# Attention summary of batches 1 to 3: exponentials transposed in blocks by VectorE, four chunks weighed over 128 rows

## The chip, the cores and the metric

One core of one Trainium2 chip. The metric is the device time of one execution in microseconds, lower is better; the figure of a kernel is the median of its runs.

## The reference

There are 4 batches of 12480 tokens with 128 channels, and 32 inducing rows that all batches share. First, in each batch, the inducing rows attend to the tokens and give a summary h of 32 rows; then the tokens attend to h. The result goes through a layer of 2048 hidden units with a piecewise quadratic in the middle.

```python
def mab(q, kv):
    s = scale * (q @ kv.transpose(0, 2, 1))
    s = s - s.max(-1, keepdims=True)
    a = np.exp(s)
    a /= a.sum(-1, keepdims=True) + 1e-09
    return a @ kv
h = mab(I, x)            # summary: (B, 32, 128)
y = mab(x, h)            # (B, 12480, 128)

h = y @ w_in             # (49920, 2048)
g = np.where(h >= 1, h, np.where(h <= -1, 0.0, (h + 1) ** 2 / 4.0))
out = g @ w_out          # (49920, 128)
```

The weights w_in and w_out come as 64-bit floats and are converted on the chip.

## The kernel before

**Chunks.** A batch is 26 chunks of 480 tokens (`chunk`). For a chunk, eight steps k each take two blocks of 128 hidden units. TensorE multiplies the attention weights `aT` with `hw`, the product of the summary and w_in, into two banks of PSUM (`hidden`, L943). ScalarE takes Relu(h+1) of it (`rise`, L951) and squares that (`square`, L937); VectorE joins the branches (`bound`, L956), which frees the banks. `rise` and `bound` do both banks in one instruction of 960 columns where the banks are neighbours and both are ready, else in two halves. In six of the eight steps (`SPLIT`) the product with w_out is taken in rounded parts: an upper part `hi` by VectorE (L979), ScalarE (L976) or GpSimd (L974), a lower part `lo` by GpSimd (L982), and three products for each block (L1008). In the other two it is one matmul in full float32. After the eight steps VectorE transposes the sum (L1020) and four DMAs store it (L1024).

**Attention of the tokens** (`attend`) runs in groups of four chunks, 32 rows of partitions for each chunk; the last group of a batch has two.

**Summary** (`summarize`) of a batch also runs in seven groups of four chunks, ahead of that batch: batch 0 at the start, batches 1 to 3 beside the chunks of the batch before. For a group of batches 1 to 3:

- `load`: one DMA for each chunk brings its tokens in rows of 120 partitions (L498, tile `xn`), and four more bring them for the transposed copy (L525, tile `xr`), which VectorE makes in blocks of 32x32 (L528).
- `score`: four matmuls give the scores of four chunks in four quadrants of 32 partitions (L547); VectorE takes the largest of each row (`most`, L552) and scales it (L555); ScalarE takes the exponentials with that offset and sums them (L564). Each chunk has an offset of its own, which the end of the summary sets right.
- `gather`: TensorE transposes the exponentials (`turn`, L588, four instructions for a group), ScalarE or VectorE evicts them (`put`, L596), sixteen matmuls weigh the tokens (`weigh`, L604), each over the 120 tokens of one chunk, and ScalarE keeps the result (`keep`, L611).
- After seven groups a chain of small steps `c1` to `c12` (L645 to L690) joins them into h.

**Order.** Nothing is ordered at run time. `Plan.order` builds the whole program as a list: every operation has a cost, a lag and a due time. The planner walks through time, and each free engine takes the ready operation with the earliest due time. Operations share slots (`SLOTS`: seven banks of PSUM `h`, tiles `xn`, `w`, `hi`, `lo` and so on). Due times are a base, such as 1950 ns for each step, plus a number from the table `DUE`. Every engine, and the queue of DMAs that SP issues, then runs its list strictly in order. Where TensorE would be idle near the start, fillers are put (`keep_on`, L1035).

**The start** loads batch 0 and both weights (L498 and L393). ScalarE, VectorE and GpSimd convert the weights, and VectorE's steps of that are L403, L406, L412, L418 and L423.

## Time and profile before

| | |
|---|---|
| median of 3 runs | 1732.89 us (1730.05 to 1733.73) |
| profiled execution | 1733.12 us, its span 1731.2 us |
| granted TensorE clock, mean | 0.996 |
| busy, share of the span | PE 98%, PEld 72%, DVE 94%, ACT 96%, POOL 94% |
| instructions | PE 8100, DVE 2123, ACT 2453, POOL 879 |

PE is TensorE's matmul, PEld its weight load, DVE VectorE, ACT ScalarE, POOL GpSimd, and SPq the queue of DMAs that SP issues. Times are from the start of the span. "Idle before" names what an engine waited for. The chain of waits goes back from the last instruction, at each step to what released it, and gives the shares of the span by engine.

### The profile page before, as it was taken

The page shows a single profiled execution, that of the slowest core. Times are in us where ns is not written, and L with a number is a line of the kernel's source. Part 1 is how long each engine was busy: PE and PEld are TensorE (multiplying, and loading weights), DVE is VectorE, ACT ScalarE, POOL GpSimd, SP SyncE. Part 2 cuts the span into 40 slices and gives each one's busy share as a digit, 9 for nine tenths or more (in the row PEclk, how much of TensorE's full clock was granted, in tenths as well). Part 3 has the DMA queues.
Part 4 walks back from the last instruction along what each step waited for, and adds up shares of the span by engine and source line. Part 5 has one row for each costly group of instructions (what it writes and reads, how often), then busy time and mean ns, then how long its engine had stood idle before and what let it go on. Part 6 is the DMA issues. An engine that isn't in the chain of part 4 may idle for free.

```text
span 1731.2 us, 26016 instructions
## 1 busy us (share of the span) xinstructions
PE 1702.3 (98%) x8100; PEld 1242.9 (72%) x8100; DVE 1625.2 (94%) x2123; ACT 1662.0 (96%) x2453; POOL 1619.2 (94%) x879
## 2 busy tenths in 40 slices
PE   7999999999999999999999999999999999999998
PEld 5777777777777777767767777777777777777776
DVE  4899999999999999999999999999999999999997
ACT  5699999999999999999999999999999999999997
POOL 1599999999899999999989999999999999999998
PEclk9899999999999999999999999999999999999999
DMA  8543334233343243342143333232212111111111
GB/s 210 136 75 69 67 60 81 48 63 62 62 83 60 51 79 65 64 80 56 36 85 63 73 65 71 51 66 52 44 27 59 35 31 29 34 35 35 34 30 18
DMA packets 427948, 105.74 MB, mean 61 GB/s; under 512 B 370562, under 2 KB 421218, under 8 KB 427810
## 3 DMA queue, kind: packets, MB, share of 16 engines
q1 hardware_dynamic: 427714, 103.96, 30.7%
q8 instruction: 64, 1.05, 0.3%
q14 instruction: 74, 0.61, 0.1%
q10 hardware_dynamic: 96, 0.13, 0.0%
HBM read 48.94 MB, written 25.56 MB: 43 GB/s over the span
## 4 chain that ended last, share of the span: by engine, by line
PE 72%; ACT 9%; DVE 8%; issue 4%; POOL 3%; DMA 2%; SPq 1%; POOLq 0%; DVEq 0%; ACTq 0%
PE banks L1008 49%; PE banks L943 16%; ACT w L951 5%; DVE w L956 4%; ACT w L937 4%; POOL lo L982 3%; DVE hi L979 2%; PE banks L604 1%; PE banks L757 1%; PE banks L547 1%; PE banks L507 1%; DMA xr<-in_x 1%; DVE oT L1020 1%; PE banks L588 1%; PE banks L1035 1%
## 5 line engine op out<-in xcount | busy, mean ns | idle before, releaser
L982 POOL TENSOR_TENSOR lo<-w,hi 128x960 fp32r<-128x960 f32 x624 | 1399.7, 2276 | 40.7 <-DVE hi L979 21.3
L956 DVE SCALAR_TENSOR_TENSOR w<-banks,w 128x480 f32<-128x480 f32 (+1 forms) x1158 | 957.0, 863 | 36.6 <-ACT w L937 30.2
L951 ACT ACTIVATE w<-banks 128x480 f32<-128x480 f32 (+1 forms) x1320 | 841.9, 711 | 16.6 <-PE banks L943 15.1
L937 ACT ACTIVATE w<-w 128x960 f32<-128x960 f32 x832 | 843.2, 1046 | 3.2
L943 PE MATMUL banks<-aT,hw 128*128 128x480 f32 x1664 | 592.3, 425 | 5.3 <-DVE w L956 3.1
L1008 PE MATMUL banks<-hi,w_lo 128*128 128x480 f32 x1248 | 520.6, 417 | 4.7 <-DVE oT L1020 3.6
L979 DVE TENSOR_REDUCE hi<-w 128x960 fp32r<-128x960 f32 x410 | 466.1, 1142 | 19.3 <-PE banks L1008 1.3
L1008 PE MATMUL banks<-hi,w_hi 128*128 128x480 f32 x1248 | 473.4, 379 | 0.0
L943 PEld LDWEIGHTS banks<-aT,hw 128*128 128x128 f32 x1664 | 305.6, 188 | 158.6 <-DVE w L956 74.0
L1008 PE MATMUL banks<-lo,w_hi 128*128 128x480 f32 x1248 | 398.8, 396 | 0.7 <-POOL lo L982 0.5
L1008 PE MATMUL banks<-w,w_f 128*128 128x480 f32 x832 | 395.3, 565 | 0.0
L1008 PEld LDWEIGHTS banks<-hi,w_lo 128*128 128x128 f32 x1248 | 234.8, 188 | 87.8 <-issue 26.4
L1008 PEld LDWEIGHTS banks<-lo,w_hi 128*128 128x128 f32 x1248 | 230.7, 188 | 73.6 <-issue 23.1
L1008 PEld LDWEIGHTS banks<-hi,w_hi 128*128 128x128 f32 x1248 | 234.7, 188 | 53.0 <-issue 22.0
L1008 PEld LDWEIGHTS banks<-w,w_f 128*128 128x128 f32 x832 | 156.1, 189 | 46.8 <-issue 27.2
L974 POOL TENSOR_SCALAR hi<-w 128x960 fp32r<-128x960 f32 x143 | 142.9, 1006 | 5.1 <-PE banks L943 1.2
L1020 DVE STREAM_TRANSPOSE oT<-banks 128x480 f32<-128x480 f32 x104 | 70.2, 675 | 9.9 <-PE banks L1008 9.5
L976 ACT CAST hi<-w 128x960 fp32r<-128x960 f32 x71 | 71.5, 1008 | 6.3 <-DVE w L956 2.3
L528 DVE STREAM_TRANSPOSE xT<-xr 128x480 f32<-128x480 f32 x78 | 51.2, 660 | 1.8 <-DMA xr<-in_x 1.8
L434 POOL TENSOR_TENSOR w_in_sb<-hi,lo 128x256 f32<-128x256 f32 x8 | 6.9, 862 | 39.8 <-DVE hi L423 39.8
L800 POOL TENSOR_TENSOR a<-a,ahi 128x480 fp32r<-128x480 f32 (+1 forms) x28 | 34.6, 1235 | 0.0
L552 DVE TENSOR_REDUCE mg<-banks 128x1 f32<-128x480 f32 (+1 forms) x28 | 18.1, 647 | 16.0 <-PE banks L547 16.0
(107 smaller groups left out, 609.7 us busy)
## 6 DMA issues: line engine op xcount, KB each, us to landing
out<-oT SPq DMA_DIRECT2D x416, 60.0 KB, 2.2
xn<-in_x SPq DMA_DIRECT2D x91, 240.0 KB, 4.4
xr<-in_x SPq DMA_DIRECT2D x312, 60.0 KB, 2.5
aT<-ahi SPq DMA_DIRECT2D x206, 60.0 KB, 2.0
aT<-a SPq DMA_DIRECT2D x206, 60.0 KB, 2.0
w<-in_moe_w_in SPq DMA_DIRECT2D x8, 256.0 KB, 3.6
w<-in_moe_w_out SPq DMA_DIRECT2D x8, 256.0 KB, 5.2
hw<-hy SPq DMA_DIRECT2D x32, 64.0 KB, 2.0
```

The costliest lines, as they stand in the source:

```text
L528: nc.vector.transpose(make(xT[b, c]), xr.tile.rearrange("c n i -> c (n i)"))
L800: nc.gpsimd.tensor_sub(a.tile.bitcast(F32R)[:rows], a.tile[:rows], a_hi.tile[:rows].bitcast(F32))
L937: nc.scalar.activation(w.tile, w.tile, AF.Square, scale=0.5)
L943: nc.tensor.matmul(make(h)[:, :CW], hw[b][ft // 4].tile[:, ft % 4 * P : (ft % 4 + 1) * P], aT[b, c].tile, start=True, stop=True,)
L951: each(of, i, hs_, w, lambda to, h: nc.scalar.activation(to, h, AF.Relu, bias=1.0))
L956: lambda to, h: nc.vector.scalar_tensor_tensor(to, h, 1.0, to, op0=ALU.max, op1=ALU.min),
L974: nc.gpsimd.tensor_scalar(make(hi), w.tile, 1.0, 0.0, op0=ALU.mult, op1=ALU.add)
L976: nc.scalar.copy(make(hi), w.tile)
L979: nc.vector.tensor_reduce(make(hi), w.tile.unsqueeze(3), axis=AX.X, op=ALU.max)
L982: nc.gpsimd.tensor_sub(make(lo), w.tile, hi.tile.bitcast(F32))
L1008: nc.tensor.matmul(acc.tile[:, :CW], wt[k][:, i, :], g.tile[:, i, :], start=first, stop=(acc.parts == 0),)
L1020: nc.vector.transpose(make(oT).rearrange("c n i -> c (n i)"), acc.tile[:, :CW])
```

## The change

It has four parts, all in batches 1 to 3 but the third and fourth.

**1. The summary of batches 1 to 3.** The tokens of the four chunks of a group are loaded into one tile, each chunk in its own 32 partitions, 15 tokens in each partition. The exponentials are transposed by VectorE in blocks of 32x32 (`over`) in place of TensorE's transposes and their eviction. Fifteen matmuls (`weigh_all`) then each weigh 128 rows, which hold tokens of all four chunks. So the four chunks need one common maximum for each inducing row. The four quadrants' maxima are moved beside each other by four DMAs of 32x1 (`line`), reduced (`one_most`) and moved back to the four quadrants by four DMAs (`spread`), and only then scaled (`less`) for the exponential. The first token loads wait for batch 0's last groups, since they share their tile with batch 0's loads.

**2. The table.** `DUE` has new numbers in nearly every line and new rows for the groups' begin (`G`) and weighing (`W`), and some assumed costs change, so the whole order is another one. The split of a step into rounded parts can be done inside PSUM in the new code (`KEPT`), but the table for it is empty and no step does so.

**3. The last chunk** splits five steps and not six (`END`).

**4. The last four stores** go two by two through the SP queue and ScalarE's queue.

```diff
+END = (0, 1, 3, 4, 6)
+KEPT = {}
 SLOTS = dict(
-    h=7, o=1, xn=9, xT=26, ...
+    h=7, o=1, xn=3, x3=9, xT=26, ...
 )
 DUE = {
-    "h": [-29500, -8350, -85150, -9450, -9450, -2350, -58850, -34750],
+    "h": [-32850, -7650, -16250, -11800, -23400, -2500, -53600, -37900],
...
+    "G": [-1550, 51230, 105810, 151540, 201470, 251300, 307230],
+    "W": [26826, 84806, 164936, 190366, 243946, 298076, 350756],
...
-KEEP = 0
+KEEP = 800
-WAIT = 181850
+WAIT = 210850
...
+    tokens = work.tile([P, SLOTS["xn"], 3 * 5 * C], F32, name="tokens")
...
 def load(g, due, step):
...
-                pool = FIRST[c % len(FIRST)] if b == 0 else "xn"
-                xn[c] = in_turn(pool) if pool == "xn" else Slot(pool)
-                got[c] = add(
-                    "SP", 700 if b else 1080, 3000, at(due, "x") if b else at(0, "x0", c),
-                    lambda c=c: nc.sync.dma_start(make(xn[c], [TP, T, C], F32), rows_of[b, c]), [], [xn[c]],
-                )
...
+                else:
+                    xn[c] = xn[c - 1] if q else in_turn("xn")
+
+                    def fetch(c=c, q=q):
+                        t = xn[c].tile or make(xn[c])
+                        nc.sync.dma_start(t[q * M : (q + 1) * M], x_cols[b, c])
+
+                    got[c] = add("SP", 700, 3000, at(due, "x"), fetch, state["first"], [xn[c]])
...
 def score(g, due):
...
             def most():
-                nc.vector.tensor_reduce(
-                    mg[:rows, g : g + 1], p1.tile[:rows, :CW], axis=AX.X, op=ALU.max
-                )
+                to = mq[:rows] if b else mg[:rows, g : g + 1]
+                nc.vector.tensor_reduce(to, p1.tile[:rows, :CW], axis=AX.X, op=ALU.max)
+                if b == 0:
+                    less()
+
+            def line(q):
+                nc.sync.dma_start(m4[:, q : q + 1], mq[q * M : (q + 1) * M])
+
+            def one_most():
+                nc.vector.tensor_reduce(m4[:, Q:], m4[:, :nq], axis=AX.X, op=ALU.max)
+
+            def spread(q):
+                nc.sync.dma_start(mg[q * M : (q + 1) * M, g : g + 1], m4[:, Q:])
+
+            def less():
                 nc.vector.tensor_scalar(nb[:rows], mg[:rows, g : g + 1], -SCALE, None, op0=ALU.mult)
...
-                    to = make(e1[g])[:rows].rearrange("w (i n) -> w i n", i=M)
-                    of = p1.tile[:rows, :CW].rearrange("w (n i) -> w i n", i=M)
+                    to, of = make(e1[g])[:rows], p1.tile[:rows, :CW]
...
+                l = [add("SP", 610, 2700, SC[1], lambda q=q: line(q), [v]) for q in range(nq)]
+                v = add("DVE", 75, 215, SC[1], one_most, l)
+                l = [add("SP", 610, 2700, SC[1], lambda q=q: spread(q), [v, prior]) for q in range(Q)]
+                mosts.extend(l)
+                v = add("DVE", 75, 215, SC[1], less, l)
...
 def gather(g, due, scored):
...
+            if b:
+                def over():
+                    to = make(eN[g], [P, NB, M])[:rows].rearrange("p n m -> p (n m)")
+                    nc.vector.transpose(to, e1[g].tile[:rows])
+
+                def weigh_all():
+                    p = make(ph)
+                    for n in range(NB):
+                        nc.tensor.matmul(
+                            p[n % Q * M : (n % Q + 1) * M, :C], eN[g].tile[:rows, n, :], xn[g * Q].tile[:rows, n, :],
+                            start=n < Q, stop=n >= NB - Q,
+                        )
+
+                def keep_all():
+                    nc.scalar.copy(hs[:, g, :], ph.tile[:, :C])
...
 def chunk(b, c):
...
+            split = k in (END if (b, c) == (B - 1, NCH - 1) else SPLIT)
...
         for k in range(Q):
-            add("SP", 640, 3000, at(due, "o") + 5000, lambda k=k: store(k), [f], [oT])
+            engine = "ACT" if (b, c) == (B - 1, NCH - 1) and k % 2 else "SP"
+            add(engine, 640, 3000, at(due, "o") + 5000,
+                lambda k=k, queue=nc.scalar if engine == "ACT" else nc.sync: store(k, queue), [f], [oT])
```

Counted over the whole order of each engine, the change has these differences: on TensorE 84 transposes of exponentials in batches 1 to 3 fewer, 315 weighing matmuls for 312 in those batches, and 68 fillers for 81; on VectorE 482 double `bound` for 506 and 700 halves for 652, 404 upper parts for 410, and six evictions of exponentials fewer; on ScalarE fifteen of these evictions fewer, 77 upper parts for 71, 339 double `rise` for 344 and 986 halves for 976; on GpSimd 623 lower parts for 624 and 142 upper parts for 143; on the SP queue 162 small DMAs more. TensorE changes 142 times between its two ways of dividing its columns after the first hidden-layer matmul, in both orders.

Three places show what moved. In them `hi`, `lo` and `w` are buffers that the start also uses for converting weights.

VectorE, in a group of batch 1, before (L552 is `most`, L555 its scaling, L956 `bound`, L979 an upper part, L528 the transposed copy, L786 a step of `attend`):

```order
L552 TENSOR_REDUCE mg<-banks 128x1
L555 TENSOR_SCALAR nb_0_118<-mg 128x1
L956 SCALAR_TENSOR_TENSOR w_1562<-banks,w_1562 128x480 x2
L979 TENSOR_REDUCE hi_1601<-w_1541 128x960
L956 SCALAR_TENSOR_TENSOR w_1585<-banks,w_1585 128x960
L786 RECIPROCAL sm_109<-sm_109 128x15
L528 STREAM_TRANSPOSE xT_1619<-xr_1418 128x480
```

The same in the change (L576 is `most`, L585 `one_most`, L591 `less`, L629 `over`, L1022 `bound`, L1080 an upper part, L550 the transposed copy, L1121 the output's transpose):

```order
L576 TENSOR_REDUCE mq_0_135<-banks 128x1
L1022 SCALAR_TENSOR_TENSOR w_1556<-banks,w_1556 128x480 x2
L1080 TENSOR_REDUCE hi_1588<-w_1530 128x960
L1022 SCALAR_TENSOR_TENSOR w_1570<-banks,w_1570 128x480 x2
L550 STREAM_TRANSPOSE xT_1608<-xr_1424 128x480
L1022 SCALAR_TENSOR_TENSOR w_1591<-banks,w_1591 128x960
L585 TENSOR_REDUCE m_1_0_136<-m_1_0_136 32x1
L550 STREAM_TRANSPOSE xT_1623<-xr_1461 128x480
L1022 SCALAR_TENSOR_TENSOR w_1597<-banks,w_1597 128x480 x2
L1080 TENSOR_REDUCE hi_1647<-w_1597 128x960
L1121 STREAM_TRANSPOSE oT_1653<-banks 128x480
L1022 SCALAR_TENSOR_TENSOR w_1630<-banks,w_1630 128x480 x2
```

The scaling stood right behind the maximum. Now five rows stand between `most` and `one_most`, five between that and `less`, which comes next.

The SP queue, at the last loads of batch 0, before (L498 loads tokens, of batch 0 where it is 96x640 and of batch 1 where it is 120x4x128; L393 loads weights):

```order
L498 DMA w_643<-in_x 96x640
L393 DMA w_663<-in_moe_w_out 128x512
L498 DMA xn_684<-in_x 120x4x128
L393 DMA w_696<-in_moe_w_out 128x512
L498 DMA xn_709<-in_x 120x4x128
L498 DMA xn_736<-in_x 120x4x128
L393 DMA w_742<-in_moe_w_in 128x512
L498 DMA xn_757<-in_x 120x4x128
L393 DMA w_768<-in_moe_w_out 128x512
L498 DMA xn_793<-in_x 120x4x128
L498 DMA xn_802<-in_x 120x4x128
L498 DMA xn_815<-in_x 120x4x128
```

The same in the change (L513 loads tokens of batch 0, L521 of batch 1, L408 weights):

```order
L408 DMA w_574<-in_moe_w_out 128x512
L513 DMA tokens<-in_x 96x640 x2
L408 DMA w_628<-in_moe_w_out 128x512
L513 DMA w_646<-in_x 96x640
L408 DMA w_664<-in_moe_w_in 128x512
L408 DMA w_678<-in_moe_w_out 128x512
L408 DMA w_720<-in_moe_w_out 128x512
L408 DMA w_751<-in_moe_w_out 128x512
L408 DMA w_806<-in_moe_w_out 128x512
L408 DMA w_817<-in_moe_w_out 128x512
L408 DMA w_856<-in_moe_w_out 128x512
L521 DMA tokens<-in_x 32x1920 x7
```

Token loads of batch 1 stood among those of w_out; now they stand behind all of them, and two loads of w_out stand ahead of the last load of batch 0.

VectorE, from the first chunk's attention weights on, before (L892 makes these weights; L403 to L423 convert w_out; L763 to L772 are steps of `attend`):

```order
L892 TENSOR_TENSOR aT_982<-banks,aT_982 64x480
L423 SCALAR_TENSOR_TENSOR hi_923<-w_882,hi_923 128x256
L406 TENSOR_SCALAR lo_999<-hi_954 128x256
L403 TENSOR_SCALAR hi_967<-hi_967 128x256
L412 SCALAR_TENSOR_TENSOR lo_999<-w_894,lo_999 128x256
L406 TENSOR_SCALAR lo_1015<-hi_967 128x256
L418 TENSOR_SCALAR hi_954<-lo_999 128x256
L763 STREAM_TRANSPOSE banks<-banks 128x480
L423 SCALAR_TENSOR_TENSOR hi_954<-w_894,hi_954 128x256
L769 TENSOR_REDUCE mx_104<-banks 128x15
L956 SCALAR_TENSOR_TENSOR w_1008<-banks,w_1008 128x960
```

The same in the change (L956 makes the weights, L1022 is `bound`, L827 to L858 are steps of `attend`):

```order
L956 TENSOR_TENSOR aT_1048<-banks,aT_1048 64x480
L827 STREAM_TRANSPOSE banks<-banks 128x480
L833 TENSOR_REDUCE mx_120<-banks 128x15
L836 TENSOR_TENSOR s_202_1084<-banks,mx_120 128x480
L844 TENSOR_REDUCE sm_121<-s_202_1084 128x15
L1022 SCALAR_TENSOR_TENSOR w_1071<-banks,w_1071 128x960
L850 RECIPROCAL sm_121<-sm_121 128x15
L1022 SCALAR_TENSOR_TENSOR w_1080<-banks,w_1080 128x960
L858 STREAM_TRANSPOSE a_1143<-s_202_1084 128x480
L1080 TENSOR_REDUCE hi_1149<-w_1080 128x960
```

The conversions that stood behind the first chunk's weights are gone from there; they stand ahead of them.

## Rows read from the trace of the kernel before

**Rows 1.** The page, parts 1 and 4: busy time, share and count; chain by engine.

```profile
PE 1702.3 (98%) x8100; PEld 1242.9 (72%) x8100; DVE 1625.2 (94%) x2123; ACT 1662.0 (96%) x2453; POOL 1619.2 (94%) x879
...
PE 72%; ACT 9%; DVE 8%; issue 4%; POOL 3%; DMA 2%; SPq 1%; POOLq 0%; DVEq 0%; ACTq 0%
```

**Rows 2.** Windows of line L943: busy time (count), clock, DMA share, GB/s.

```profile
385.00:785.00 400.00, 140.40 (x397) 72.88 (x397) 1.00 0.35 66
1300.00:1700.00 400.00, 153.20 (x422) 77.14 (x420) 1.00 0.18 34
```

**Rows 3.** Timeline of TensorE: start us, us, engine, line, operation, count.

```profile
704.49 0.38 PE L1008 MATMUL banks<-hi,w_hi 128*128 128x480 f32 x1
704.71 0.60 PE L588 MATMUL banks<-ident,e 128*120 128x128 f32 x4
705.06 0.46 PE L1008 MATMUL banks<-lo,w_hi 128*128 128x480 f32 x1
...
711.69 1.08 PE L604 MATMUL banks<-xn,eN 120*32 120x128 f32 x32
712.70 0.48 PE L943 MATMUL banks<-aT,hw 128*128 128x480 f32 x1
```

**Rows 4.** Groups by line and form: count, busy us, mean ns, idle before.

```profile
L956 DVE SCALAR_TENSOR_TENSOR w<-banks,w 128x960 f32<-128x960 f32 x506 | 569.6, 1145 | 27.4 <-ACT w L937 23.0 <-POOL hi L974 2.1 <-issue 0.4
L951 ACT ACTIVATE w<-banks 128x480 f32<-128x480 f32 x976 | 531.6, 609 | 15.8 <-PE banks L943 14.7
...
L979 DVE TENSOR_REDUCE hi<-w 128x960 fp32r<-128x960 f32 x410 | 466.1, 1142 | 19.3 <-PE banks L1008 1.3 <-DVE w L956 0.5 <-POOL lo L982 0.3
...
L956 DVE SCALAR_TENSOR_TENSOR w<-banks,w 128x480 f32<-128x480 f32 x652 | 395.5, 645 | 9.2 <-ACT w L937 7.3
...
L951 ACT ACTIVATE w<-banks 128x960 f32<-128x960 f32 x344 | 339.8, 1001 | 0.8 <-PE banks L943 0.4
...
L976 ACT CAST hi<-w 128x960 fp32r<-128x960 f32 x71 | 71.5, 1008 | 6.3 <-DVE w L956 2.3 <-PE banks L1008 2.1 <-POOL w_lo L470 0.8
...
L794 DVE STREAM_TRANSPOSE a<-s 128x480 f32<-128x480 f32 x24 | 16.0, 667 | 1.4 <-DMA aT<-a 1.2 <-POOL s L789 0.2
...
L596 ACT COPY eN<-banks 120x512 f32<-120x512 f32 x12 | 7.7, 642 | 0.0
...
L596 DVE COPY eN<-banks 120x512 f32<-120x512 f32 x6 | 3.9, 656 | 0.0
...
L645 DVE TENSOR_REDUCE m<-mg 128x1 f32<-128x7 f32 x4 | 0.6, 142 | 0.0
```

**Rows 5.** Timeline of the end, GpSimd, TensorE and the SP queue.

```profile
1715.67 8.87 POOL L982 TENSOR_TENSOR lo<-w,hi 128x960 fp32r<-128x960 f32 x4
...
1716.79 1.77 PE L1008 MATMUL banks<-w,w_f 128*128 128x480 f32 x4
...
1726.03 2.58 SPq L1024 DMA_DIRECT2D out<-oT  x4
```

**Rows 6.** The page, part 6: DMA issues, count, KB each, us to landing.

```profile
aT<-ahi SPq DMA_DIRECT2D x206, 60.0 KB, 2.0
...
w<-in_moe_w_out SPq DMA_DIRECT2D x8, 256.0 KB, 5.2
```

**Rows 7.** Waits, of the SP queue and of TensorE: us, times, longest us.

```profile
SPq L1024 <- DVE oT L1020: 411.8, 49, 12.1
...
PEld banks L943 <- DVE w L956: 74.0, 220, 1.0
```

**Rows 8.** Chain from 66 to 75 us, first and last of eight conversions.

```profile
66.57 0.68 DVE hi L423
...
72.73 1.12 DVE lo L412
```

**Rows 9.** Window 40 to 60 us, all engines: PE, PEld, DVE, ACT, POOL.

```profile
40.00:60.00 20.00, 18.61 (x197) 13.80 (x197) 13.90 (x47) 8.70 (x26) 5.22 (x7) 0.77 0.89 216
```

**Rows 10.** Timeline of ScalarE at 50 us, with the wait ahead.

```profile
49.94 0.43 ACT L398 ACTIVATE hi<-w 128x256 f32<-128x256 f32 x1 [1.45 <-DMA w<-in_moe_w_out]
```

131 lines of the change are left out of this document (89 added, 42 removed), and 56 rows, old and new, of the table DUE.

## The prediction

> **What bounds the kernel now.** I read the page's busy shares and its chain of waits first. TensorE is busy 98% of the span and 72% of the chain runs through it; ScalarE has 9% of the chain, VectorE 8%, GpSimd 3% [rows 1]. So a microsecond taken off TensorE is worth most, but the three elementwise engines are nearly full too (94 to 96%), and a saving that only moves work among them is worth little.
>
> Then I asked what the summary of the next batch costs where it runs. The windows of line L943 count hidden-layer matmuls, 16 to a chunk. In 400 us of batches 1 and 2, where each batch's chunks run beside the summary of the next, there are 397 of them, 16.12 us a chunk; in 400 us of batch 3, which has no summary beside it, 422, or 15.17 us a chunk [rows 2]. That is 0.95 us for each of the 78 chunks of batches 0 to 2, 74 us in all, or 3.5 us for each of the 21 groups of later batches. This is the pot that the change can draw from.
>
> **The steady stretch.** *TensorE loses* the transposes of the exponentials: the four of one group begin at 704.71 and the next matmul at 705.06, so 0.35 us, and 21 groups make 7.35 us. The weighing of a full group is 16 matmuls (32 records) from 711.69 to 712.70, 1.01 us or 0.063 each [rows 3]. It becomes 15 matmuls: 18 full groups save 1.1 us, and the three groups of two chunks go from 8 to 15 and lose 1.3. Net 7.1 us less on TensorE. At TensorE's share of the chain, 0.72, I take **−5.1 us**.
>
> *VectorE gains* a transpose of the exponentials in each group. The nearest row is the other 128x480 transpose between two buffers of SBUF, 667 ns: 21 make 14.0 us. One small maximum per group is nearest to the 142 ns reduction of seven columns: 3.0 us. It loses the six evictions that it did, 656 ns each: 3.9 us. In the whole order, bounding falls from 506 to 482 double instructions and rises from 652 to 700 halves: 48 x 0.645 − 24 x 1.145 = 3.5 us more. Upper parts fall from 410 to 404, 6.9 us less [rows 4]. Net +9.7 us, at 8% of the chain **+0.8**. *ScalarE* loses twelve evictions of 642 ns and three of half the size, 8.7 us; it gains six upper parts of 1.0 us, and ten halves of Relu at 609 ns for five doubles at 1.0 [rows 4]: net −1.6 us, **−0.1**. The exponential's stepped read becomes a straight one, which I cost at nothing. *GpSimd* does one lower part (2.2 us [rows 5]) and one upper part (about 1.0, as on ScalarE) fewer, **−0.1**.
>
> *The round trip.* A group's maximum now goes through the SP queue and back, and 21 groups issue 78 plus 84 small transfers. The nearest issues take 0.645 us each (four stores in 2.58 [rows 5]), the nearest landing is 2.0 us, for a copy between two buffers of the chip [rows 6]. Three issues, and the landing of the fourth, make 3 x 0.645 + 2.0 = 3.9 us, twice in each group. What stands between the two ends on VectorE covers it: at the group shown above, two bounds in halves, an upper part, a transpose and a double bound, 4 x 0.645 + 1.14 + 0.67 + 1.15 = 5.5 us, and as many rows stand there on the way back. So I cost the waits at **0**. If that cover is gone, VectorE stands still in program order, and the next bounds, which free TensorE's banks, come late. The scores' bank is held for two such trips longer, some 10 us; its cost I see in the halves counted above. 162 issues are 104 us more for SP, which stands 412 us in front of the output's transpose alone, in 49 waits [rows 7]; that is the cover. The token loads stay 78, and nothing waits for them in the rows I read.
>
> Steady stretch: −5.1 + 0.8 − 0.1 − 0.1 = **−4.5 us**. The best end takes TensorE's saving at its share of what a group costs: scores as long as the weighing, 0.35 of 2.37 us is 15%, of 74 us −11.0. The worst end takes the elementwise engines alone: (9.7 − 1.6 − 3.2)/3 = +1.6. I stay at the chain's shares, since the chain is the only row that weighs all four engines.
>
> **The start.** In the chain from 66 to 75 us VectorE still converts w_out, between the first chunk's attention weights and the first bounds: eight pieces, the first 0.68 us and the last 1.12, together 4.4 [rows 8]. By the order no such conversion is left behind the first chunk's weights: **−4.4**. They move into a time when VectorE is busy for 13.9 of 20 us, so the 6.1 that are idle cover them [rows 9]. They can, because the nine token loads of batch 1 that stood among the w_out loads now stand behind them. But two of the w_out loads also stand ahead of the last token load of batch 0. At 256 KB each [rows 6] and the 216 GB/s of that stretch [rows 9] they are 2.4 us of transfer, and I put them on the path: **+2.4**. In return the conversion that held up ScalarE for 1.45 us for its w_out transfer [rows 10], with the exponential of the batch's sum behind it, should find its data there: **−1.5**. The 13 fewer fillers on TensorE cost and give nothing, since they stand in its idle time. Start: **−3.5**; bounds +2.4 (conversions hidden anyway) and −5.9 (loads not on the path).
>
> **The end.** Four lower parts run back to back on GpSimd from 1715.67, 2.2 us each; behind the last come two matmuls, a transpose and four stores in a row on one queue [rows 5]. With one lower part fewer GpSimd is done 2.2 us sooner. Behind its last lower part TensorE now has one matmul in full float32 left, 0.9 us (two of them took 1.77 [rows 5]), and four with the upper part, 0.9 us at the 0.22 between two of them [rows 3]. Two of the four stores go to ScalarE's queue, 2 x 0.645 = 1.3 us. End: −2.2 + 1.8 − 1.3 = **−1.7 us**, bounds 0 and −3.5.
>
> **Sum.** −4.5 − 3.5 − 1.7 = −9.7 us. The profiled execution took 1733.1 us (its span is 1731.2), 0.2 above the median of three, 1732.9, so I do not shift it: **1723 us**.
>
> **Rivals.**
> (1) *TensorE is not the bound.* Its matmul records overlap, so 98% overstates it; its weight loads are busy for 72% [rows 1]. Then the steady stretch gets the elementwise sum, +1.6: 1733.1 + 1.6 − 3.5 − 1.7 = 1729.5. For it speaks that all three are above 93%; against it the 72% of the chain, which follows releases and not busy time. Chance 0.18. The Trainium skill's page "Perfetto Trace Analysis" (Identifying the Most-Contended Engine) says that matmul busy time is no measure of TensorE's headroom and that weight-load time is one to read; by it the time would be this rival's 1729.5 and not 1723.
> (2) *The summary costs what its parts on TensorE suggest*: −11.0 in the steady stretch, 1716.9. For it: a group costs 3.5 us of span, more than its 2.4 on TensorE. Against it: what else the group does stays. Chance 0.12.
> (3) *The start gives nothing*: conversions hidden anyway, loads on the path, 1733.1 − 4.5 + 2.4 − 1.7 = 1729.3. Against it: eight conversions lie in the chain. Chance 0.07.
> (4) *Slower: VectorE waits for the round trip.* Place: the small maximum and the scaling, 42 waits in VectorE's order. The cover is 5.5 us against 3.9, but the trip begins only when SP is free, and SP stands in front of one store for up to 12.1 us; and TensorE's weight loads already wait 74 us, 220 times, for the bounds [rows 7]. With a mean wait of 0.23 us the gain is gone, above 0.32 the kernel is slower by over 0.2%; at 0.6 us it is 1723 + 25 = 1748. Against it: 1.6 us of slack each time. Chance 0.14. The Trainium skill's page "DMA: Bandwidth & Descriptors" (Specifications) says that below 512 B a transfer is read, changed and written back; by it these pieces of 4 bytes, of which no row here has any, take longer than my 3.9 us.
> (5) *A bank short*: 21 x 10 us on six banks of seven is a seventh of 210, 30 us if all of it tells; half of it gives 1738. Chance 0.04.
>
> **How the numbers follow.** The forecast keeps 0.45. A measurement here can tell about 0.2% from no change, 3.5 us. Faster by more (below 1729.4): 0.44 of the forecast, all of rival 2, and half of rivals 1 and 3, which lie on that line, some 0.13: in all 0.69. Within it: the other half, 0.12, 0.01 of the forecast and 0.04 for mild forms of rivals 4 and 5: 0.17. Slower: the rest of 4 and 5, 0.14. The range 1712 to 1736 takes in rivals 1 to 3 and the bounds of start and end; it leaves out the slow side, 0.14, and a little below.
>
> **What would show it.** Right: no transposes of exponentials in batches 1 to 3, and a chunk in batches 1 and 2 at about 16.06 us by the count of hidden-layer matmuls; no conversion of w_out on VectorE behind the first weights; the last store issued some 1.3 us sooner after the last transpose. Wrong: VectorE's small maximum or its scaling waiting for DMA by 10 us or more in all; TensorE waiting longer for the bounds than its 74 us; weight conversions that hold up the batch's sum.

## The result: 1736.7 us, slower by 0.2%

The changed kernel takes **1736.67 us** (median of 10 runs, 1735.27 to 1738.55) beside 1732.47 us for the old one in the same comparison (10 runs, 1730.05 to 1734.49). The ratio is 1.0022 with a 95% interval of 1.0014 to 1.0031, so 2.4 to 5.4 us more. The forecast was 1723.0 us, and the result lies outside its range of 1712 to 1736. The profiled execution took 1737.56 us with a span of 1735.8, 4.6 above the old span.

The profile after, busy time and chain of the page (for [rows 1]):

```profile
PE 1700.5 (98%) x7994; PEld 1225.6 (71%) x7994; DVE 1626.9 (94%) x2178; ACT 1663.0 (96%) x2450; POOL 1614.3 (93%) x876
...
PE 68%; DVE 12%; ACT 10%; issue 4%; DMA 2%; SPq 2%; POOL 1%; DVEq 0%; ACTq 0%; POOLq 0%
```

TensorE is busy for 1.8 us less, where 7.1 us of its work had gone by the forecast's count. This row tells little: in the profiles of kernels with these same 7994 TensorE instructions it lies anywhere from 1696.2 (best2, below) to 1702.3 us (tok_late).

Every chunk's output is turned once by VectorE (line L1020 before, L1121 after), so the n-th such row of two traces tells how far one is behind the other. The timelines of VectorE and TensorE, old kernel first: sum of batch 0, first hidden-layer matmul, first projecting matmul, output of the first, fourth and last chunk.

```profile
50.80 0.16 DVE L668 TENSOR_REDUCE tot<-fs 128x1 f32<-128x7 f32 x1
66.60 0.71 PE L943 MATMUL banks<-aT,hw 128*128 128x480 f32 x2
85.59 0.49 PE L1008 MATMUL banks<-hi,w_lo 128*128 128x480 f32 x1
100.23 0.67 DVE L1020 STREAM_TRANSPOSE oT<-banks 128x480 f32<-128x480 f32 x1
147.49 0.67 DVE L1020 STREAM_TRANSPOSE oT<-banks 128x480 f32<-128x480 f32 x1
1725.32 0.68 DVE L1020 STREAM_TRANSPOSE oT<-banks 128x480 f32<-128x480 f32 x1 [5.33 <-PE banks L1008]
```

The same in the changed kernel:

```profile
57.90 0.16 DVE L732 TENSOR_REDUCE tot<-fs 128x1 f32<-128x7 f32 x1
73.62 1.11 PE L1009 MATMUL banks<-aT,hw 128*128 128x480 f32 x4 [0.69 <-DMA hw<-hy]
82.00 0.46 PE L1109 MATMUL banks<-hi,w_lo 128*128 128x480 f32 x1
103.58 0.64 DVE L1121 STREAM_TRANSPOSE oT<-banks 128x480 f32<-128x480 f32 x1
155.11 0.67 DVE L1121 STREAM_TRANSPOSE oT<-banks 128x480 f32<-128x480 f32 x1
1730.60 0.68 DVE L1121 STREAM_TRANSPOSE oT<-banks 128x480 f32<-128x480 f32 x1 [4.74 <-PE banks L1109]
```

The differences, in order: +7.1, +7.0, −3.6, +3.4, +7.6, +5.3, and +4.6 at the end of the span. So **the start lost 7.6 us** by the fourth chunk, **the 100 chunks behind it gave back 2.3**, and what follows the last chunk's output 0.7. The forecast had −3.5, −4.5 and −1.7. One profile of a start is good to a microsecond or two. Three profiles have the old kernel's order up to the first hidden matmul, which comes at 65.3 to 66.6 us in them, and seven have the changed one's, with 70.9 to 73.6, so the changed profile shown is the latest of its kind. The lag at the fourth chunk is 6 us or more whichever two are set beside each other.

Three readings go with this. First, **the loss grows in two places**: up to the first hidden layer (+7.0), and between the first projection and the fourth chunk's output (from −3.6 to +7.6). Batch 0's first and last scores, old kernel, with the maximum behind the last:

```profile
15.06 1.83 PE L547 MATMUL banks<-xT,indT 128*32 128x480 f32 x8 [0.28 <-DVE indT L367]
...
44.20 1.00 PE L547 MATMUL banks<-xT,indT 128*32 128x480 f32 x4
...
45.36 0.64 DVE L552 TENSOR_REDUCE mg<-banks 64x1 f32<-64x480 f32 x1
```

In the changed kernel the first begin 6.3 us later, so most of the loss is there already. The last begin at 52.49, 8.3 us later, behind the weighing of another group, and VectorE stands in front of the maximum with a conversion of w_out:

```profile
21.38 1.83 PE L570 MATMUL banks<-xT,indT 128*32 128x480 f32 x8 [0.28 <-DVE indT L382]
...
52.70 0.98 PE L570 MATMUL banks<-xT,indT 128*32 128x480 f32 x6
...
53.31 0.83 DVE L446 TENSOR_TENSOR hi<-hi,lo 128x256 f32<-128x256 f32 x1
54.07 0.65 DVE L576 TENSOR_REDUCE mg<-banks 128x1 f32<-128x480 f32 x1
```

Second, **SP's queue in the ramp carries what it did not carry before**: twelve token loads of batch 1 between 58 and 104 us, where the old kernel issues none between 52 and 104. Some rows of it (start, time, number of issues last):

```profile
58.91 3.56 SPq L521 DMA_DIRECT2D tokens<-in_x  x7
...
78.41 5.32 SPq L547 DMA_DIRECT2D xr<-in_x  x8
83.77 1.07 SPq L521 DMA_DIRECT2D tokens<-in_x  x2
...
96.25 1.20 SPq L887 DMA_DIRECT2D aT<-ahi  x2
97.55 2.59 SPq L547 DMA_DIRECT2D xr<-in_x  x4
100.19 1.25 SPq L887 DMA_DIRECT2D aT<-a  x2
```

Right ahead of the last copies shown stand four x loads, no token load. For these copies VectorE waits before it may write the attention's weights `a` anew (waits of VectorE from 80 to 175 us; the old kernel has no such row there):

```profile
DVE a L858 <- DMA aT<-a: 2.9, 2, 2.2
```

Third, **the round trip costs no wait** (the collecting transfers' line: landing, least, median, most; then the small maximum's line, its wait in the whole run; the scaling behind the spreading transfers has no wait at all):

```profile
DMA to landing us min/median/max: 1.6/1.7/3.5
...
  DMA m<-mq: 0.2, 1
```

### The profile page after: what moved, and what is told of

The parts are those of the page before. It is cut to its first block, busy times and chain, and to the rows that moved or that the text cites. A ratio compares the mean times of both kernels' runs of the same rounds, so it can differ in the third digit from the quotient of the medians.

```text
span 1735.8 us, 26095 instructions
## 1 busy us (share of the span) xinstructions
PE 1700.5 (98%) x7994; PEld 1225.6 (71%) x7994; DVE 1626.9 (94%) x2178; ACT 1663.0 (96%) x2450; POOL 1614.3 (93%) x876
## 4 chain that ended last, share of the span: by engine, by line
PE 68%; DVE 12%; ACT 10%; issue 4%; DMA 2%; SPq 2%; POOL 1%; DVEq 0%; ACTq 0%; POOLq 0%
PE banks L1109 48%; PE banks L1009 15%; DVE w L1022 6%; ACT w L1017 5%; ACT w L1003 4%; DVE hi L1080 3%; PE banks L570 1%; PE banks L634 1%; DVE oT L1121 1%; POOL lo L1083 1%; PE banks L821 1%; SPq L547 1%; ACT hi L1077 1%; DMA w<-in_x 0%; DMA ind_sb<-in_inducing 0%
## 5 line engine op out<-in xcount | busy, mean ns | idle before, releaser
L1022 DVE SCALAR_TENSOR_TENSOR w<-banks,w 128x480 f32<-128x480 f32 (+1 forms) x1182 | 958.7, 848 | 42.9 <-ACT w L1003 37.4
L1017 ACT ACTIVATE w<-banks 128x480 f32<-128x480 f32 (+1 forms) x1325 | 839.9, 701 | 17.6 <-PE banks L1009 15.8
L1009 PE MATMUL banks<-aT,hw 128*128 128x480 f32 x1664 | 585.8, 422 | 5.4 <-DVE w L1022 2.5
L1080 DVE TENSOR_REDUCE hi<-w 128x960 fp32r<-128x960 f32 x404 | 457.9, 1140 | 12.9 <-PE banks L1109 2.0
L1109 PE MATMUL banks<-lo,w_hi 128*128 128x480 f32 x1246 | 407.3, 401 | 1.0 <-POOL lo L1083 0.8
L1077 ACT CAST hi<-w 128x960 fp32r<-128x960 f32 x77 | 77.1, 1001 | 2.1 <-PE banks L1109 1.1
L1121 DVE STREAM_TRANSPOSE oT<-banks 128x480 f32<-128x480 f32 x104 | 70.1, 674 | 8.8 <-PE banks L1109 8.0
L550 DVE STREAM_TRANSPOSE xT<-xr 128x480 f32<-128x480 f32 x78 | 51.0, 657 | 0.0
L570 PE MATMUL banks<-xT,indT 128*32 128x480 f32 x208 | 30.8, 611 | 0.5 <-DVE indT L382 0.3
```

The costliest lines, as they stand in the source:

```text
L550: nc.vector.transpose(make(xT[b, c]), xr.tile.rearrange("c n i -> c (n i)"))
L570: nc.tensor.matmul(p[q * M : (q + 1) * M, :CW], indT, xT[b, c].tile, start=True, stop=True)
L1009: nc.tensor.matmul(make(h)[:, :CW], hw[b][ft // 4].tile[:, ft % 4 * P : (ft % 4 + 1) * P], aT[b, c].tile, start=True, stop=True,)
L1017: each(of, i, hs_, lambda h, to: nc.scalar.activation(to, h, AF.Relu, bias=1.0), w)
L1022: lambda h, t: nc.vector.scalar_tensor_tensor(h if kept else t, h, 1.0, t, op0=ALU.max, op1=ALU.min), w,
L1077: nc.scalar.copy(make(hi), w.tile)
```

## The experiments

All times are ratios to the old kernel run on the same chip beside each, with the 95% interval; 0.001 is 1.7 us, and the changed kernel stands at 1.0022. Kernels whose first part is that of the changed one have the fourth chunk's output at 153.6 to 155.4 us in their profiles, so a shift of a microsecond there is no evidence by itself. The times of two runs whose intervals overlap are not told apart either; that holds for nearly all single moves below beside the changed kernel's 1.0014 to 1.0031.

**The start's order as a whole, both ways.** The change rewrites the table for the start too, and not for batches 1 to 3 alone. `old_start` is the changed kernel with eleven rows of the table of due times (wi, wc, wo, oc, A0, A1, e0, x0, t0, s0, g0) as before; `new_start` is the old kernel with those rows of the change.

> The changed kernel, with its summaries as the change makes them, but with the due times of the start (weights, conversions, inducing points, batch 0's tokens, scores and gather) as they were before the change. Theory A, that the whole loss is made by the order of the start and the steady stretch still gains 2.5 to 3 us: the output transpose of chunk 3 comes back from 155.1 to about 147.5 us, the lag behind the old kernel turns to a lead of some 3 us by chunk 75, and the time is 1727 to 1730 us. Theory B, that the loss comes from the new summaries themselves (later batches run without the room that the old start left): chunk 3's transpose stays over 151 us and the time is 1733 us or more.

Measured 1.0212 (1.0198 to 1.0225), 1770.7 us. The fourth chunk's output comes at 145.66, 1.8 us *ahead* of the old kernel, but that is no gain: up to there TensorE has made 64 hidden-layer matmuls, those of the four chunks, where the old and the changed kernel have 76 and 78, most of the fifth chunk among them. Windows of the hidden layer's line up to the fourth output, old_start, changed and old kernel:

```profile
60.00:145.66 85.66, 22.41 (x64) 11.89 (x64) 0.96 0.38 78
```

```profile
60.00:155.11 95.11, 27.06 (x78) 14.84 (x79) 0.96 0.51 102
```

```profile
60.00:147.49 87.49, 27.97 (x76) 13.86 (x77) 0.99 0.44 83
```

The fifth chunk had no attention weights yet, and TensorE stands still for their copy:

```profile
145.55 2.92 PE L821 MATMUL banks<-xT,hT 128*32 128x480 f32 x24
160.65 1.94 PE L1009 MATMUL banks<-aT,hw 128*128 128x480 f32 x4 [12.18 <-DMA aT<-a]
```

The fifth chunk is 24.7 us late, and the last 38.9. Theory B's time came true, but this run decides nothing about the start: where a table of due times sets the order, putting rows back moves everything behind them as well.

> The converse: the old kernel with all its summaries as they were, but with the due times of the start that the change brings. Theory A, that the order of the start alone costs what the two traces show (chunk 3's output transpose 7.6 us later): the time is 6 to 9 us above the old kernel, 1738 to 1742 us. Theory B, that the new start costs only together with the new summaries: within 2 us of 1732.5 us.

Measured 1.0071 (1.0053 to 1.0088). Neither theory: the sum is as late as in the changed kernel (56.11 us), but the first hidden matmul comes at 68.04, the fourth output at 145.91, 1.6 us ahead of the old kernel and with as many hidden matmuls done (76). The loss, 7.8 us at the last output of its profiled execution, comes later, 4.5 of it between the outputs that the old kernel has at 1484.6 and 1545.4. So neither a late sum nor these eleven rows make the start's loss by themselves. Only two token loads stand in its ramp.

**Single pieces of the start**, in the changed kernel's own order, so that nothing else moves (`old_conv` alone is planned anew).

`ind_first`:

```diff
     done = plan.order()
+    done.remove(ind_in)
+    done.insert(0, ind_in)
```

> The changed kernel with one instruction moved: the load of the inducing points stands first among all the work again, so its DMA is issued before the tokens' loads of batch 0 and not after some of them (13.65 us with the change, 6.05 before). Theory A, that the late load sets the start: the first scores come at about 15 us in place of 21.4, and with the rest of the order as it is the time falls by 3 to 6 us, to 1731 to 1734 us. Theory B, that the start is set by what stands on the engines behind it (the eight conversions of w_out in the chain of batch 0's summary): the first scores come earlier all the same, but the last scores of batch 0 and the first chunk's output transpose move by under 1 us, and the time stays within 1.5 us of 1736.7 us.

Measured 1.0009 (1.0000 to 1.0017): 1 to 2 us below the changed kernel. Its first scores come at 19.25 and not at the 15 of theory A; with the load in its late place they come at 19.4 to 22.0 in the profiles here. aT_first below, with the late load, has its last scores at the same 49.5 us. The load is at most a small part.

`tok_late`; `both` adds the lines of ind_first:

```diff
+    late = [got_all[1, c] for c in range(7)]
+    for op in late:
+        done.remove(op)
+    n = max(done.index(op) for op in hw_made[0][-1]) + 1
+    done[n:n] = late
```

> The changed kernel with the first seven token loads of batch 1 (240 KB each, issued in a row from 58.91 us, just ahead of the copies of hw over the partitions) moved behind the last of those copies on SP's queue; nothing else moves. Theory C, that these loads hold up the copies of hw and with them the first hidden layer (73.6 us with the change, 66.6 before): the first hidden matmul comes 3 to 5 us sooner, chunk 3's output transpose (155.1 us) 3 us or more, and the time falls by 3 to 5 us against the changed kernel, to 1732 to 1735 us. Theory B, that the conversions of w_out in front of the batch's sum make the start: under 1 us in all of these, and within 1.5 us of the changed kernel.

Measured 1.0039 (1.0025 to 1.0053), 2.9 us above the changed kernel. The first hidden matmul did come at 69.77 in place of 73.62, but the fourth output at 157.39: the seven loads now stand ahead of the x loads and of the attention's copies.

> The changed kernel with the inducing points' load first (which alone moved chunk 3's transpose from 155.1 to 154.1 us) and the seven token loads of batch 1 behind the copies of hw. If the two act one after the other, the gains add: some 1 us more than the run with the token loads alone. If the loads of the attention's transposed copies, which stand behind the next batch's loads on SP's queue between 80 and 130 us, hold the first chunks up instead, the first hidden matmul comes early but chunk 3's transpose stays above 152 us, and the time within 2 us of the changed kernel.

Measured 1.0029 (1.0020 to 1.0039). The first hidden matmul is at 66.79, as early as in the old kernel, and the fourth output still at 154.63. So an early first hidden layer does not bring the fourth chunk by itself, with the seven loads ahead of the x loads and the copies; the second branch of the expectation came true.

`aT_first` (`k` is the first place behind the work that the copy needs and the last use of its buffer):

```diff
+    for c in range(1, 12):
+        for op in sorted(aT_made[0, c], key=done.index):
...
+            del done[i]
+            done.insert(k, op)
```

> The changed kernel with the attention's transposed copies of chunks 1 to 11 moved ahead on SP's queue, to right behind the work that makes their data; the next batch's loads that stood ahead of them (four x loads before chunk 2's, eight before chunk 4's) come behind them. Theory D, that these loads hold the copies up, and with them VectorE, which waits 2.2 us at 103 us and 0.8 us at 164 us before it may overwrite their source: VectorE's waits for them go, chunk 4's output transpose (171.1 us) comes 2 to 4 us sooner and the time falls by as much, to 1733 to 1735 us. Theory B, that the first chunks are late because of the chain up to batch 0's sum: within 1.5 us of the changed kernel.

Measured 1.0005 (0.9995 to 1.0014), nearly 3 us below the changed kernel. VectorE's row of 2.9 us for `aT<-a` is gone between 80 and 175 us (one wait of 2.2 us for an x load takes its place), and the fourth output comes at 152.87. Theory D, for a part of the loss.

`old_conv`:

```diff
-    "wo": [-98550, 139851, 23902, 221503, 193654, -65395, 424906, 245107],
-    "oc": [-100150, -148450, -101050, -110750, -141750, -12150, 132150, -20900],
+    "wo": [-37700, 167201, 19502, 211153, 217354, -10995, 418206, 226207],
+    "oc": [-208900, -172800, -130600, -189550, -129050, -59750, 12900, -119800],
```

> The changed kernel with only the due times of w_out as they were (its loads and its conversions, two rows of the table); the conversions then stand again between and behind the first chunk's attention, and not all ahead of batch 0's sum. Theory B, that the conversions in front of the sum make the start's loss: the sum of the exponentials' row, at 57.9 us with the change, comes 3 us or more sooner, chunk 3's output transpose (155.1 us) falls below 151 us, and the time with it, to 1731 to 1733 us. Theory D, that the loss is made behind it, where the next batch's loads and the attention's copies share SP's queue between 78 and 165 us: chunk 3 within 2 us of 155.1, the time within 2 us of the changed kernel (1736.7 us).

Measured 1.0125 (1.0109 to 1.0140). The sum comes at 54.13 and the fourth output at 151.48, 3.6 us sooner, which speaks for the conversions' place; but this order is planned anew behind it and loses another 19 us on the old kernel by the last chunk, so that the time says nothing of the start.

`out_behind`:

```diff
+    z = max(done.index(got_all[0, c]) for c in range(NCH))
+    early = [op for op in done[:z] if op in OUT_LOAD]
...
+    done = [op for op in done[: z + 1] if op not in early] + early + done[z + 1 :]
```

> The changed kernel with the two loads of w_out that stand ahead of batch 0's last four token loads moved right behind them on SP's queue; nothing else moves. Theory L, that these loads hold up the last scores, as the forecast's +2.4 us assumed: the last scores (49.3 to 52.5 us in the profiles of this order so far) and the first hidden layer (70.9 to 73.6) come 2 to 3 us sooner and the time falls by 1 to 3 us, to 1734 to 1736 us. Rival, that the order on TensorE and the elementwise engines holds them: under 1 us in the time, within 1.5 us of 1736.7.

Measured 1.0017 (1.0008 to 1.0027), 0.9 us below the changed kernel, the first hidden matmul at 71.46. That is within the noise, and the forecast's +2.4 us for these loads does not show. In the changed kernel the last token load of batch 0 lands at 43.5 us, 9.0 ahead of the last scores.

`sum_first` (`k` as in aT_first):

```diff
+    final = max((m for m, _, _ in GROUPS), key=done.index)
+    line = [op for ops in GROUPS if ops[0] is final for op in ops] + CHAIN
+    for op in line:
...
+        del done[i]
+        done.insert(k, op)
```

> The changed kernel with one group of batch 0 moved up: the scores, maximum and exponential of the group that comes last, and the chain of the batch's sum behind them, stand right behind the work they need, ahead of the weighing of two other groups on TensorE and of some conversions of w_out on VectorE. Nothing else moves. Theory E, that this order makes the start: the last scores stood at 52.5 us with the change (44.2 before), behind the weighing; they come 3 to 5 us sooner, the sum with them (57.9 us), the first chunk's output transpose 2 to 4 us, and the time falls by 2 to 4 us, to 1733 to 1735 us. Theory D, that SP's queue behind 78 us makes it: the sum comes sooner, but chunk 3's output transpose (155.1 us) by under 1 us, and the time stays within 1.5 us of the changed kernel.

Measured 1.0026 (1.0015 to 1.0037): nothing. The last scores come at 49.94, the sum at 56.10, the first hidden matmul at 74.41, the fourth output at 156.88.

**Three moves together** (ind_first, sum_first and aT_first), and with the w_out loads a fourth:

> The changed kernel with three moves together: the inducing load first, the last group of batch 0 with the sum's chain ahead of the weighing, and the attention's transposed copies of chunks 1 to 11 ahead of the next batch's loads. If each gives what it gave or is expected to give alone (1, 2 to 4 and 1.5 us) and they add, the time is 1730 to 1732 us, 1 to 3 us below the old kernel. If they act on the same wait, it is 1733 to 1735 us.

Measured 1.0002 (0.9993 to 1.0010), 1733.2 us: 3.5 us below the changed kernel and clear of its interval, level with the old one. The fourth output is at 151.29, half of the 7.6 us won back.

> The version with the three moves (inducing load first, last group and sum ahead, attention's copies ahead; level with the old kernel at 1733.2 us) with the two w_out loads behind batch 0's last token loads too. If the loads' gain adds: 1730 to 1732 us, below the old kernel. If not: 1733 us again.

Measured 1.0004 (0.9995 to 1.0013). It does not add, and its fourth output is at 154.41. No version that beats the old kernel was found.

**What TensorE's work is worth**, in four kernels. `more_turns` (at the head of `weigh_all`):

```diff
                     p = make(ph)
+                    for t in range(4):
+                        nc.tensor.transpose(
+                            p[:120, t * P : t * P + rows], e1[g].tile[:rows, t * 120 : (t + 1) * 120],
+                            ident[:rows, :rows],
+                        )
```

> The changed kernel with the four TensorE transposes of each group's exponentials put back, 84 in all over the 21 groups; their results are written into the bank that the weighted sums take afterwards and are read by nobody. At 0.35 us for the four of a group they are 7.35 us of TensorE. Theory A, as forecast, that TensorE bounds the steady stretch and 72% of such work is on its chain: the time rises by 4 to 6 us, to 1741 to 1743 us. Theory B, that the saving was covered by waits of the other engines: under 1.5 us more. In between (2 to 3 us) the steady gain read from the lags, 2.5 to 3 us, is what the transposes are worth and the forecast's share was too high.

Measured 1.0073 (1.0061 to 1.0085), 8.8 us above the changed kernel for 7.35 us of work, more than any branch of the expectation. The group of the transposes, here and (second) in turns_before:

```profile
L634 PE MATMUL banks<-ident,e 128*120 128x128 f32 x72 | 10.8, 273 | 0.0
```

```profile
L588 PE MATMUL banks<-ident,e 128*120 128x128 f32 x144 | 18.6, 272 | 0.0
```

`light_after`:

```diff
-                    for n in range(NB):
+                    for n in [0, 1, 2, 3, 11, 12, 13, 14]:
```

> The changed kernel with 7 of the 15 weighing matmuls left out in each of the 21 groups of later batches (the output is then not the reference's); 7 x 0.066 us of TensorE in a group, 9.7 us in all, and nothing else changes. Putting 7.35 us of transposes back cost 9 us. Theory P, that TensorE bounds the changed kernel still: the time falls by 7 us or more, below 1730 us. Theory K, that the kernel stands at the kink, where TensorE's saving from the change has already uncovered the three elementwise engines: it falls by 3 us at most.

Measured 1.0017 (1.0008 to 1.0027): 0.9 us less, within the interval of nothing. Theory K.

`light_before` (in `weigh`):

```diff
-                for t in range(T):
+                for t in range(T) if b == 0 else (0, T - 1):
```

> The old kernel with half of the weighing matmuls left out in the later batches (8 of 16 in a full group at 0.066 us, 10.3 us of TensorE in all); the output is then not the reference's. It asks of the old kernel what the forecast assumed of it. Theory P, that TensorE bounds it for 72% or more of such work: the time falls by 7 us or more, to 1726 us or less. Theory K, that it stood at the kink already: by 3 us at most, 1729.5 us or more; then the forecast's 5.1 us for 7.1 us of TensorE were never to be had by taking work off TensorE alone.

Measured 0.9981 (0.9972 to 0.9990): 3.3 us less for 10.3 us of work, at the edge of theory K. Its profiled execution, the slowest of its eleven, shows none of it where the matmuls were left out: from the fourth output to the last it takes 1578.5 us, the old kernel 1577.8. So a third is the most that the saving gave.

`turns_before` (in `turn`):

```diff
-                for t in range(T):
+                for t in range(T) if b == 0 else [*range(T), *range(T)]:
```

> The old kernel with each of the 84 transposes of the exponentials in the later batches made twice, 7.35 us more of TensorE. In the changed kernel these cost 9 us, and in the old one 10.3 us less gave 3. Theory K, that both kernels stand at the kink (all engines planned to end together in a fixed order): the time rises by 5 us or more here too, to 1739 us or more. Rival, that the old kernel had room on TensorE and only the changed one is full: under 3 us more.

Measured 1.0052 (1.0040 to 1.0064), 9.0 us more for 7.35. That is theory K. Both kernels pay in full, and more, for work added to TensorE, and get a third or nothing for work taken away.

**The new parts of the summary.**

`no_trip` (the same return stands in `one_most` and `spread`):

```diff
-                to = mq[:rows] if b else mg[:rows, g : g + 1]
+                to = mq[:rows] if b and nq < Q else mg[:rows, g : g + 1]
...
             def line(q):
+                if nq == Q:
+                    return
```

> The changed kernel without the round trip of the maxima in the 18 groups of four chunks: each quadrant keeps its own maximum, written where the shared one would stand; the collecting transfers, the small maximum and the spreading transfers of these groups are not issued (144 transfers and 18 small instructions of VectorE). It leaves out the common maximum, so the sums are not the reference's. Putting the transposes back cost some 9 us, while the steady stretch gained only 2 to 3 us between chunks 3 and 75, so that something new costs some 6 us there. Theory T, that it is the trip (VectorE's wait, SP's issues, the banks held longer): the time falls by 4 us or more, to 1733 us or less. Theory V, that VectorE's own new work costs it: within 1.5 us of the changed kernel.

Measured 1.0017 (1.0008 to 1.0026), 0.9 us below the changed kernel. Theory T falls.

`no_over`:

```diff
-                    nc.vector.transpose(to, e1[g].tile[:rows])
...
-                            p[n % Q * M : (n % Q + 1) * M, :C], eN[g].tile[:rows, n, :], xn[g * Q].tile[:rows, n, :],
+                            p[n % Q * M : (n % Q + 1) * M, :C], e[:rows, n, :], xn[g * Q].tile[:rows, n, :],
```

> The changed kernel without the 21 turnings of the exponentials on VectorE (657 ns each, 13.8 us): the weighed sums read the exponentials as they lie. It leaves the turning out, so its sums are not the reference's. Theory V, that the steady stretch's missing 6 us are VectorE's, where the transposes went that TensorE lost: the time falls by 4 us or more, to 1733 us or less, and TensorE's weight loads wait less for VectorE's output copies (30.1 us) and upper parts (8.2 us). Theory T, that the round trip costs them: under 1.5 us.

Measured 1.0024 (1.0015 to 1.0033): nothing, with VectorE at 1617.4 us busy. TensorE's weight loads wait as long as before for the output copies and the upper parts:

```profile
PEld banks L1109 <- DVE oT L1121: 30.6, 68, 3.2
PEld banks L1109 <- POOL lo L1083: 26.4, 80, 1.0
...
PEld banks L1109 <- DVE hi L1080: 8.6, 25, 1.0
```

Theory V falls too. `light_both` leaves out what light_after and no_over leave out:

> The changed kernel with 7 of 15 weighing matmuls and the turning of the exponentials on VectorE left out in the 21 later groups: 9.7 us less of TensorE and 13.8 us less of VectorE (the output is not the reference's). Each alone changed the time by under 1 us. If VectorE holds when TensorE is relieved (or the other way round), the two together give 4 us or more, to 1733 us or less. If it is ScalarE and GpSimd, whose work is untouched at 96 and 93%, the time stays within 2 us of the changed kernel.

Measured 1.0015 (1.0007 to 1.0024), 1.2 us below the changed kernel. Neither TensorE nor VectorE nor both hold it; ScalarE and GpSimd were not relieved in any run, so that they do is left as argued.

## Why the forecast was wrong

**The start: −3.5 forecast, +7.6 measured. This is the step that failed.** Of the 7.6 us, 7.0 are there at the first hidden matmul, when nothing of the new summaries has run but seven token loads, so that part is made by the start's order and its loads. That the eleven rows of the start are enough for it is not shown: new_start, which has them with the old summaries, is at the fourth chunk where the old kernel is. The order changed by more than these rows, and the sum of the forecast has three terms for it. Two are not what failed: the exponential behind the transfer (−1.5) came as forecast, since from the last maximum to the sum the changed kernel takes 3.8 us for 5.4, and the two w_out loads (+2.4) do not show. Ahead of the last scores the forecast had that +2.4 and nothing else, and they come 8.3 us later. Three sentences of the prediction bear on this.

"By the order no such conversion is left behind the first chunk's weights: −4.4" holds as far as it goes: from the first hidden matmul to the first projection the changed kernel needs 8.4 us in place of 19.0. But the first output is not nearer for it: the first projection comes 3.6 us sooner and the first output 3.4 later. The conversions lay in the chain of [rows 8], and what stands next behind them was not asked for. In the window from the first projection to the first output (length, then busy time of TensorE, its weight loads, VectorE, ScalarE, GpSimd) it is GpSimd that is full, with 20.9 us of work where the old kernel has 13.0 in the 14.6 of this stretch:

```profile
82.00:103.60 21.60, 17.35 (x72) 11.12 (x70) 18.56 (x27) 18.96 (x30) 20.86 (x13) 1.00 0.60 119
```

"They move into a time when VectorE is busy for 13.9 of 20 us, so the 6.1 that are idle cover them" looked at one engine's idle time over 20 us and not at the order around it. VectorE from 50 to 60 us (third busy time), old and changed kernel:

```profile
50.00:60.00 10.00, 8.98 (x46) 7.08 (x46) 6.27 (x23) 2.19 (x7) 1.57 (x2) 0.55 0.85 216
```

```profile
50.00:60.00 10.00, 9.80 (x127) 7.88 (x126) 9.59 (x32) 6.14 (x21) 4.41 (x5) 1.00 0.26 72
```

In these ten of the twenty 0.4 us are idle now, where it was 3.7, and the chain of the changed kernel runs through conversions of weights on both sides of the sum at 57.90, which the prediction had named as a sign of being wrong. Some pieces of it:

```profile
50.91 0.42 DVE lo L427
...
53.90 0.41 ACT w_f L478
54.33 0.44 ACT hi L413
...
58.06 0.85 DVE lo L427
```

From the sum to the first hidden matmul the two kernels take the same (15.8 and 15.7 us), from the last maximum to the sum the changed one takes less, as said; the 7 us are lost ahead of that, 6.3 of them ahead of the first scores, and the last scores now stand behind another group's weighing. That the conversions cause it is not shown: they hold the last maximum for 0.4 us and its exponential, on ScalarE, for another 0.4 (54.90 to 55.28), old_conv's last scores are as late (49.65), and sum_first, which moves the scores ahead, gave nothing.

"The nine token loads of batch 1 that stood among the w_out loads now stand behind them" was seen, and priced at nothing. These loads land in the ramp, on a queue that issues with hardly a gap from 71 to 104 us, and the attention's copies stand behind the next batch's loads. aT_first shows some 3 us for the copies' place, at the edge of the noise; tok_late and both show that a load moved out of one jam goes into the next.

**What stays open:** the three moves of best account for 3.5 us of the time. The rest of the start's 7.6, and what makes the first scores late, could not be put down to one instruction or transfer: no single move gave more than 3 us, and putting rows back (old_conv, old_start) plans everything behind them anew.

**The steady stretch: −4.5 forecast, −2.3 measured; sign right, price wrong.** The pieces are as worked out: 84 transposes gone, VectorE's turning 657 ns each as its row said (667), exponentials 675 ns. In 400 us of batches 1 and 2 there are 400 hidden matmuls for the 397 of [rows 2], 16.0 us a chunk where 16.06 was forecast, and 420 for the 422 in batch 3:

```profile
385.00:785.00 400.00, 139.22 (x400) 72.99 (x401) 1.00 0.34 65
1300.00:1700.00 400.00, 155.12 (x420) 77.09 (x420) 1.00 0.17 34
```

The failed step is "At TensorE's share of the chain, 0.72, I take −5.1". A share of the chain is no exchange rate. The runs have the rate for more work at 1.2 (8.8 and 9.0 us for 7.35) and for less at 0.3 or below (3.3 for 10.3, 0.9 for 9.7), with the work worked out from their spacing in the traces (0.35 us for four transposes, 0.066 for a weighing matmul). Waits of TensorE's weight loads show where a saved microsecond goes; old kernel (beside the 74.0 us for the bounds of [rows 7]):

```profile
PEld banks L1008 <- DVE oT L1020: 23.2, 67, 1.2
PEld banks L1008 <- POOL lo L982: 18.8, 45, 0.9
```

Changed kernel:

```profile
PEld banks L1009 <- DVE w L1022: 64.3, 199, 0.8
...
PEld banks L1109 <- DVE oT L1121: 30.1, 68, 3.2
PEld banks L1109 <- POOL lo L1083: 26.0, 79, 1.0
```

It waits 9.7 us less for bounds and 14.1 more for output copies and lower parts.

**The end: −1.7 forecast, −0.7 measured.** GpSimd, TensorE, SP's and ScalarE's queue at the end:

```profile
1724.94 2.22 POOL L1083 TENSOR_TENSOR lo<-w,hi 128x960 fp32r<-128x960 f32 x1 [0.47 <-DVE hi L1080]
...
1728.72 0.96 PE L1109 MATMUL banks<-w,w_f 128*128 128x480 f32 x2
...
1731.31 1.24 SPq L1125 DMA_DIRECT2D out<-oT  x2
...
1731.32 1.52 ACTq L1125 DMA_DIRECT2D out<-oT  x2
```

GpSimd is done 3.4 us before the last turning (1727.16 to 1730.60) where it was done 0.8 before ([rows 5]: 1724.54 to 1725.32), so 2.6 us sooner by the clock of the last chunk, where 2.2 were forecast; but the work behind it took those 2.6 back, where the forecast had 1.8. The last store is issued 2.2 us behind the turning in place of 3.3: 1.1 of the 1.3 forecast, of which 0.7 is left at the end of the span.

**The rivals.** Rival 1 (TensorE is not the bound) has a reason that is half right: a saving on TensorE is worth little, but TensorE has no room upward either. Its +1.6 for the steady stretch is farther from the −2.3 measured than the forecast's −4.5. The Trainium skill's page "Perfetto Trace Analysis" (Identifying the Most-Contended Engine) says that matmul busy time does not tell how near the limit TensorE is. The profiles agree: with the same 7994 instructions the busy time differs by up to 6.1 us, nearly as much as the 6.3 by which it fell in light_before. The weight loads' share, one of two measures that the page recommends instead, is 72% in the old kernel and would have promised room, and turns_before shows none. Rival 3 (the start gives nothing) had the right place and too small a size. Rival 4 (the round trip) is ruled out by a wait of 0.2 us in all and by no_trip. In its page "DMA: Bandwidth & Descriptors" (Specifications) the Trainium skill says that below 512 B a transfer is read, changed and written back; the pieces of this trip landed in 1.7 us at the median, where copies of 60 KB took 2.0 [rows 6], so here that cost nothing that was seen. Rival 5 (a bank short) was not tried by itself. The forecast gave a slower kernel a chance of 0.14 and laid all of it on rivals 4 and 5: it has come out slower by another way. All four of the prediction's signs of being right came true, since none of them looks at the start ahead of the first chunk's weights.

## What to carry to other kernels

In a kernel with a fixed order in which every engine is busy for 93 to 98% of the span, ask of each saving what happens in both directions: a run with work doubled and one with work left out cost little and tell the rate, which was 1.2 for more and 0.3 or less for less; the share of the chain told neither. Idle time of an engine covers moved work only if its place in the program order lies in that idle time; look which rows it stands in front of, and how much is idle just there. And when a change moves loads, follow the queue through the next 50 us: what leaves one stretch of it arrives in another, and here one such place was worth some 3 us, where the whole steady gain was 2.3. Last, an early output shows a gain only beside the work that was done by then: old_start's fourth output was early because the fifth chunk had not begun.

## What had not been expected of the hardware

Transfers of 128 bytes in 32 rows, from one buffer of the chip to another, land in 1.6 to 3.5 us, no later than those of 60 KB (1.9 to 3.9). And the busy time of TensorE in a profile does not follow its work to a few microseconds: 9.7 us of matmuls left out of the changed kernel lowered it from 1700.5 to 1697.6, and kernels with all their matmuls have 1696.2 to 1702.3.
